# Decode attention with a gated FFN on one core: the output weights in three pieces instead of four, and unread matmuls moved

## The chip, the cores and the metric

The kernel runs on one core of a Trainium2 chip. The metric is the device time of one execution in microseconds; the time of a kernel is the median of several runs.

## What is computed

One decode step for two sequences: a layer norm, attention over the last 2048 positions of a cache, and a feed-forward network (FFN) whose output gates the attention's.

```
xn = layernorm(x)                                  # 2 x 1 x 448
q = (xn @ wq) -> 16 heads of 256
k, v = the last W = 2048 rows of the 8 kv heads, each used by 2 query heads
p = softmax(q k^T * 256**-0.5)
s = (p v) -> 2 x 1 x 4096 @ wo                     # wo is 4096 x 448
g = silu(relu(xn @ w1) @ w2)                       # 448 -> 1792 -> 448
out = x + s * g
```

Nearly all the bytes are the keys and values (eight loads of 4 MB), then wq and wo (3.67 MB each) and w1 and w2 (1.6 MB each).

## The kernel before, in words

Every engine has a list of operations written out by hand (`pr.op`, `pr.dma`); a wait stands in front of an operation only where it names another as a dependency. TensorE's list is cut into sections, which a small program of branches (L126 to L163) strings together: SA and SB (the scores), PV (probabilities times values), OT (the output turned), CH (the softmax chain), and at the end FFN, PV and OT once more, WO and END.

The work goes in four turns, k = 0 to 3. In each, the keys of one quarter of the heads are loaded (`load_k`), turned on VectorE in eight pieces (`do_T`, L460) and multiplied into the PSUM bank sbk by 32 matmuls (`do_S`). The softmax chain follows (L508 to L532), then 32 matmuls with the values (`do_PV`, into obk), a scaled copy to o_sb on ScalarE, and four small matmuls that turn it (`do_oT`).

All loads but two small ones are issued on SyncE's one queue, in the order wq, keys and values in turns, w1, w2, the last values, and then wo. wo goes into the buffer of the keys of turns 0 and 2 (`wo_sb = kbuf[0]`). A row of wo here is one of 32 slices: the 4096 rows are laid out as 128 partitions with 32 rows of 448 each, so that each of the 32 is one matmul's moving operand, 112 KB. `WO_PARTS` says in how many loads they come, `landed` which row has to wait for which load.

The end of the kernel, in TensorE's order: section FFN has two halves of the first product (`do_H`, 7 matmuls each into fbk and cbk), whose results VectorE takes through relu, a transpose and copies into h_sb (`do_hT`), and 14 matmuls with w2 (`do_F`); ScalarE and VectorE then make the gate g_sb (`do_gate`). The last PV and OT follow. In section WO two small matmuls fold the heads (`m_at`) and VectorE copies the result to at2. The first `WO_WIDE` rows of wo are multiplied wide: 448 columns each, four at a time in four strips of 32 columns of the array, so that four partial sums lie in wbk. VectorE copies wbk to wsum (L630), and four matmuls with `sel` add the four strips up into cbk. The remaining rows are multiplied narrow (`narrow`): each as four matmuls of 112 columns, in four strips, straight into cbk. The rows of the last load are in section END. Two VectorE operations multiply by the gate and add x, and ScalarE's queue stores the result.

`keep_busy(bank, n)` (L491) is a matmul in fp32 of the identity with n columns of itself, which runs as two matmuls. Nobody reads what it writes, and it waits for nothing: an unread matmul. Before the change there are such matmuls in each OT (256 columns, into wbk), behind the fold of the heads (512, into sbk), behind the first load's wide matmuls (384), and behind the last wide one (256).

Line 382 in the profile is the helper that makes all ordinary matmuls, L492 the unread ones, L46 the loads.

Of the kernel before, what the change touches and what calls it, by code (L numbers as in the profile page):

```python
# [165 lines left out]
def bass_recurrent_scan__sliding_block_cached__dense_activation_relu__decode_kernel(  # L166
# [24 lines left out]
    SLOTS = 7  # L191
    HC = HD // 2
    FC = DFF // 2
    WO_PARTS = [18, 6, 6, 2]
    WO_WIDE = 24
    NCOL = D // 4
    QW = 24 + 8 * 128
    BIG = 1e30
# [2 lines left out]
    with es:  # L201
# [5 lines left out]
        def psum(name, shape, dt):  # L207
            return es.enter_context(nc.psum_tensor(name, shape, dt))

        def view(t, off, dims, n=128, p0=0, pstep=1):  # L210
            width = t.shape[1]
            return bass.AP(t, p0 * width + off, [[width * pstep, n]] + dims)
# [55 lines left out]
        sbk = psum("sbk", [128, 512], F32)  # L268
# [112 lines left out]
        def mm(out_ap, lhsT, rhs, start, stop=False, **kw):  # L381
            return lambda e: e.matmul(out_ap, lhsT=lhsT, rhs=rhs, start=start, stop=stop,  # L382
                                      skip_group_check=True, **kw)
# [26 lines left out]
        def do_H(u):  # L410
            deps = [d_w1, v_xw] if u == 0 else []
            for s in range(SLOTS):
                lo = s * FC + u * (FC // 2)
                o = pr.op(PE, mm((fbk, cbk)[u][0:4, 0:FC // 2], xr[:, 4 * s:4 * s + 4], wbuf[:, lo:lo + FC // 2],
                                 s == 0, s == SLOTS - 1), deps)
                deps = []
            st["h_n"] = pr.op(DVE, lambda e: e.tensor_scalar(
                out=view(h_n, 32 * u, [[64, 14], [1, 32]], n=4), in0=view((fbk, cbk)[u], 0, [[1, 14], [14, 32]], n=4),
                scalar1=0.0, scalar2=None, op0=ALU.max), [o, p_z])

        def do_hT(u):
            v = pr.op(DVE, lambda e: e.transpose(
                view(ht, 32 * u, [[64, 14], [1, 32]], n=32), view(h_n, 32 * u, [[64, 14], [1, 32]], n=32)),
                [st["h_n"]])
            for hf in range(2):
                st["hT"] = pr.op(DVE, lambda e, hf=hf: e.tensor_copy(  # L426
                    view(h_sb, 0, [[1, 14], [16, 2]], n=32, p0=64 * hf + 32 * u),
                    view(ht, 32 * u + hf, [[64, 14], [2, 2]], n=32)), [v, p_z])

        def do_F():  # L430
            deps = [d_w2, st["hT"]]
            for f in range(14):
                lo = W2 + f * D
                o = pr.op(PE, mm(fbk[0:17, 0:D], h_sb[:, f:f + 17], wbuf[:, lo:lo + D], f == 0, f == 13), deps)
                deps = []
            st["F"] = o

        def do_gate():
            for i in range(4):
                a_e = pr.op(ACTE, lambda e, i=i: e.activation(  # L440
                    ea[32 * i:32 * i + 17, :], fbk[0:17, i * NCOL:(i + 1) * NCOL], ACT.Exp, scale=-1.0),
                    [st["F"], p_z])
            for i in range(4):
                a_g = pr.op(ACTE, lambda e, i=i: e.activation(
                    ga[32 * i:32 * i + 17, :], fbk[0:17, i * NCOL:(i + 1) * NCOL], ACT.Copy))
            v_d = pr.op(DVE, lambda e: e.tensor_scalar(
                out=ea[:, :], in0=ea[:, :], scalar1=1.0, scalar2=None, op0=ALU.add), [a_e])
            v_rc = pr.op(DVE, lambda e: e.reciprocal(tmp[:, :], ea[:, :]), [v_d])
            st["g"] = pr.op(DVE, lambda e: e.tensor_tensor(
                out=g_sb[:, :], in0=ga[:, :], in1=tmp[:, :], op=ALU.mult), [v_rc, a_g])  # L450
# [40 lines left out]
        def keep_busy(bank, n):  # L491
            pr.op(PE, lambda e: e.matmul(bank[:, 0:n], lhsT=ident_f[:, :],  # L492
                                         rhs=view(ident_f, 0, [[0, n // 128], [1, 128]]), start=True, stop=True))
# [100 lines left out]
        landed, j0 = {}, 0  # L594
        for n in WO_PARTS:
            landed[j0] = pr.dma(SP, wo_sb[:, j0 * D:(j0 + n) * D], wo_src[:, j0 * D:(j0 + n) * D],
# [5 lines left out]
        do_hT(0)  # L602
        do_H(1)
        do_hT(1)
        do_F()
        do_gate()
        pr.section("PV", NQ)
# [6 lines left out]
        for b in range(2):  # L614
            m_at = pr.op(PE, mm(mbk[:, 256 + 32 * b:288 + 32 * b], at_exp[:, 128 * b:128 * b + 128],
                                fold[:, :], b == 0, b == 1), deps)
            deps = []
        keep_busy(sbk, 512)
        v_at2 = pr.op(DVE, lambda e: e.tensor_copy(at2[:, :], mbk[:, 256:320]), [m_at])
        deps = [v_at2]  # L620
        for j in range(WO_WIDE):
            i = j % 4
            m_w = pr.op(PE, mm(wbk[32 * i:32 * i + 2, 0:D], view(at2, j, [[32, 2]]), wo_sb[:, j * D:(j + 1) * D],
                               j < 4, j + 4 >= WO_WIDE, tile_position=(0, 32 * i)), deps + [landed.get(j)])
            deps = []
            if j == WO_PARTS[0] - 1:
                keep_busy(sbk, 384)
            if j == WO_WIDE - 1:
                keep_busy(sbk, 256)
        v_ws = pr.op(DVE, lambda e: e.tensor_copy(wsum[:, :], wbk[:, 0:D]), [m_w])  # L630
# [11 lines left out]
        for i in range(4):  # L642
            pr.op(PE, mm(cbk[32 * i:32 * i + 17, 0:NCOL], sel[:, :], wsum[:, i * NCOL:(i + 1) * NCOL],
                         True, tile_position=(0, 32 * i)), deps)
            deps = []
        for j in range(WO_WIDE, 32):
            if j == max(landed):
# [39 lines left out]
```

## Time and profile before

| | |
|---|---|
| median of 3 runs | 110.13 us (109.85 to 110.47) |
| the profiled execution | 109.7 us, span of its instructions 108.4 us |
| mean granted clock of TensorE | 0.89 of full |
| busy: TensorE, VectorE, ScalarE, GpSimd | 69.6, 62.2, 14.9, 7.9 us |
| read from memory | 44.11 MB, 407 GB/s over the span |

The profile is of one execution; its times start at the span's first instruction. In a row of the timeline the columns are start, length, engine, line, operation, output and inputs with their shapes, and how many such instructions the row takes together; in brackets stands how long the engine was idle before it, and what ended that. A row of a table of stretches has the stretch and its length, then the busy time of PE, PEld, DVE, ACT and POOL with the number of instructions, the granted clock of TensorE, the busy share of the DMA engines and GB/s. In the list of DMA issues the last column is the median time from issue to landing.

### The profile page before, as it was taken

The numbers are of one execution on the slowest core, as the hardware profiler recorded it, in microseconds if no ns is written. First come the engines' busy times: TensorE is split into PE (matmuls) and PEld (weight loads), VectorE is DVE, ScalarE is ACT, GpSimd is POOL, SyncE is SP. The second block draws the span as 40 slices with busy tenths as digits, with TensorE's granted clock in tenths as the row PEclk, the third lists the DMA queues.
The fourth block names the chain that finished last, engine by engine and source line by source line (L and its number), as shares of the span: only waits on it lengthen the run. The fifth ranks groups of instructions, "written<-read, shape, count | busy, mean of one in ns | idle before, by whom it ended". The sixth has DMA issues, their size and how long they took to land.

```text
span 108.4 us, 1147 instructions
## 1 busy us (share of the span) xinstructions
PE 69.6 (64%) x432; PEld 27.4 (25%) x432; DVE 62.2 (57%) x106; ACT 14.9 (14%) x33; POOL 7.9 (7%) x31
## 2 busy tenths in 40 slices
PE   0000940059982999963799993169996597578891
PEld 0000200023421433432233332023432331223240
DVE  1679078099948999043999313299942216404022
ACT  2991000000003000203000023000002300045000
POOL 6500023000012000030000020000000000000000
PEclk9999999999999959999558999556999755999999
DMA  2999998899899998999889988998899998899970
GB/s 58 451 447 401 520 447 387 387 496 472 387 387 472 496 387 387 399 508 447 387 387 508 460 387 387 435 532 387 387 384 431 503 447 387 387 444 417 397 291 1
DMA packets 2332, 44.11 MB, mean 407 GB/s; under 512 B 282, under 2 KB 412, under 8 KB 668
## 3 DMA queue, kind: packets, MB, share of 16 engines
q1 hardware_dynamic: 2304, 44.11, 95.2%
q10 hardware_dynamic: 28, 0.01, 0.1%
HBM read 44.11 MB, written 0.00 MB: 407 GB/s over the span
## 4 chain that ended last, share of the span: by engine, by line
DMA 60%; PE 29%; DVE 5%; SPq 2%; issue 1%; ACT 1%; DVEq 0%; ACTq 0%
DMA kbuf<-in_A_k_cache_dram 42%; PE sbk L382 22%; DMA kbuf<-in_A_wo_dram 18%; PE obk L382 3%; DVE kt L460 2%; SPq L46 2%; PE wbk L382 1%; PE cbk L382 1%; PE sbk L492 1%; ACT e_sb L526 1%; DVE rm L508 1%; DVE wsum L630 1%; PE mbk L382 0%; PE nbk L382 0%; DVE mx L517 0%
## 5 line engine op out<-in xcount | busy, mean ns | idle before, releaser
L382 PE MATMUL sbk<-kt,qbd 128*128 128x512 bf16 x128 | 37.0, 456 | 12.7 <-DVE kt L460 12.7
L460 DVE STREAM_TRANSPOSE kt<-kbuf 128x1024 f32<-128x1024 f32 x32 | 36.7, 1206 | 6.8 <-DMA kbuf<-in_A_k_cache_dram 6.8
L382 PEld LDWEIGHTS sbk<-kt,qbd 128*128 128x128 bf16 x128 | 13.7, 111 | 35.3 <-issue 24.1
L382 PE MATMUL fbk<-wbuf,xq 128*4 128x512 bf16 x28 | 3.2, 624 | 10.9 <-DVE xq L369 10.9
L405 POOL COPY qbd<-qt 32x64 bf16<-32x64 bf16 x16 | 4.5, 284 | 54.4 <-PE sbk L382 42.5
L382 PE MATMUL obk<-vbuf,pt 128*16 128x512 bf16 x128 | 7.6, 379 | 0.8 <-DMA vbuf<-in_A_v_cache_dram 0.8
L488 ACT ACTIVATE o_sb<-obk,rs 128x512 bf16<-128x512 f32 x4 | 2.8, 688 | 37.5 <-PE obk L382 36.9
L508 DVE TENSOR_REDUCE rm<-sbk 128x1 f32<-128x512 f32 x4 | 2.8, 692 | 7.9 <-PE sbk L382 7.9
L525 ACT ACTIVATE bias<-mbk 128x1 f32<-128x1 f32 x4 | 0.7, 171 | 33.9 <-PE mbk L382 33.9
L382 PE MATMUL nbk<-ssum,gsum 128*128 128x1 f32 x8 | 1.7, 286 | 4.5 <-ACT e_sb L526 4.5
L531 DVE STREAM_TRANSPOSE pt<-e_sb 128x512 bf16<-128x512 bf16 x4 | 2.7, 687 | 3.2 <-ACT e_sb L526 3.2
L382 PEld LDWEIGHTS obk<-vbuf,pt 128*16 128x16 bf16 x128 | 2.8, 89 | 5.3 <-issue 1.3
L535 DVE TENSOR_TENSOR at_exp<-nbk,qmask 128x64 bf16<-128x64 f32 x4 | 0.9, 222 | 5.6 <-PE nbk L382 5.6
L382 PE MATMUL fbk<-wbuf,h_sb 128*17 128x448 bf16 x14 | 2.8, 352 | 2.0 <-DVE h_sb L426 2.0
L382 PEld LDWEIGHTS fbk<-wbuf,xq 128*4 128x4 bf16 x28 | 0.8, 107 | 12.4 <-issue 11.8
L382 PE MATMUL mbk<-one_f,mrow 1*128 1x1 f32 x8 | 1.5, 256 | 2.8 <-DVE mrow L520 2.8
L359 DVE TENSOR_SCALAR xg<-x_sb,st,rstd 2x384 bf16<-2x384 bf16 (+2 forms) x5 | 2.9, 603 | 0.1
L382 PE MATMUL cbk<-wbuf,xr 128*4 128x448 bf16 x7 | 2.8, 577 | 0.0
L526 ACT ACTIVATE e_sb<-sbk,bias 128x512 bf16<-128x512 f32 x4 | 2.7, 687 | 0.4
L382 PE MATMUL fbk<-wbuf,xr 128*4 128x448 bf16 x7 | 2.8, 571 | 0.0
L492 PE MATMUL sbk<-ident_f 128*128 128x512 f32 (+2 forms) x6 | 2.7, 534 | 0.0
L630 DVE COPY wsum<-wbk 128x448 f32<-128x448 f32 x1 | 0.6, 625 | 3.6 <-PE wbk L382 3.6
(85 smaller groups left out, 50.4 us busy)
## 6 DMA issues: line engine op xcount, KB each, us to landing
kbuf<-in_A_k_cache_dram SPq DMA_DIRECT2D x4, 4096.0 KB, 23.0
vbuf<-in_A_v_cache_dram SPq DMA_DIRECT2D x4, 4096.0 KB
wbuf<-in_B_w_dram SPq DMA_DIRECT2D x2, 1568.0 KB, 20.6
wbuf<-in_A_wq_dram SPq DMA_DIRECT2D x1, 2560.0 KB, 10.5
kbuf<-in_A_wo_dram SPq DMA_DIRECT2D x1, 2016.0 KB, 19.0
kbuf<-in_A_wo_dram SPq DMA_DIRECT2D x2, 672.0 KB, 20.7
wbuf<-in_A_wq_dram SPq DMA_DIRECT2D x1, 1024.0 KB, 4.8
kbuf<-in_A_wo_dram SPq DMA_DIRECT2D x1, 224.0 KB, 21.3
```

What stands on the lines that cost most here:

```text
L46: o = _Op(eng, lambda e: e.dma_start(dst, src), deps, True, key)
L359: xs["xn"] = pr.op(DVE, lambda e: e.tensor_scalar(out=view(xg, 128 + 128 * lo + shift, [[256, blocks], [128, 2], [pairs, 128 // pairs]], n=B),
L382: return lambda e: e.matmul(out_ap, lhsT=lhsT, rhs=rhs, start=start, stop=stop, skip_group_check=True, **kw)
L405: st["qbd", k] = pr.op(POOL, lambda e, a=a: e.tensor_copy(view(qbd, 24 + 32 * a, [[128, 8], [2, 4], [1, 2]], n=32, p0=32 * a), view(qt, 0, ...
L460: st["T", k, e] = pr.op(DVE, lambda e: e.transpose(view(dst, lo, [[128, NT // 2], [1, 32]]), view(src, lo, [[128, NT // 2], [1, 32]])), de ...
L488: st["osb", k] = pr.op(ACTE, lambda e: e.activation(o_sb[:, :], obk[:, :], ACT.Copy, scale=rs[:, k:k + 1]), [st["PV", k], st["rs", k]], ke ...
L492: pr.op(PE, lambda e: e.matmul(bank[:, 0:n], lhsT=ident_f[:, :], rhs=view(ident_f, 0, [[0, n // 128], [1, 128]]), start=True, stop=True))
L508: st["rm", k] = pr.op(DVE, lambda e: e.tensor_reduce(out=rm[:, :], in_=sbk[:, :], axis=AX.X, op=ALU.max), [st["S", k, 7]], key="rm")
L526: st["exp", k] = pr.op(ACTE, lambda e: e.activation(e_sb[:, :], sbk[:, :], ACT.Exp, bias=bias[:, 0:1], accum_out=ssum[:, 0:1]), [a], key=" ...
L531: st["pt", k] = pr.op(DVE, lambda e: e.transpose(pt[:, :], e_sb[:, :]), [st["exp", k]], key="pt")
L535: st["at", k] = pr.op(DVE, lambda e: e.tensor_tensor(out=view(at_exp, 16 * k, [[64, 4], [4, 4], [1, 4]]), in0=view(nbk, 0, [[4, 4], [1, 4] ...
L630: v_ws = pr.op(DVE, lambda e: e.tensor_copy(wsum[:, :], wbk[:, 0:D]), [m_w])
```

## The change

The loads of wo become three, of 22, 8 and 2 rows, and the 22 rows of the first are the wide ones; rows 22 and 23 become narrow. The unread matmul of 384 columns between the wide ones is gone. Behind the fold of the heads there are two unread matmuls of 512 columns instead of one, and two new ones, of 512 and 256 columns into sbk, stand in front of the second product of the FFN.

```
-    WO_PARTS = [18, 6, 6, 2]
-    WO_WIDE = 24
+    WO_PARTS = [22, 8, 2]
+    WO_WIDE = 22
...
         do_hT(0)
         do_H(1)
         do_hT(1)
+        for n in (512, 256):
+            keep_busy(sbk, n)
         do_F()
...
-        keep_busy(sbk, 512)
+        for n in (512, 512):
+            keep_busy(sbk, n)
         v_at2 = pr.op(DVE, lambda e: e.tensor_copy(at2[:, :], mbk[:, 256:320]), [m_at])
...
             deps = []
-            if j == WO_PARTS[0] - 1:
-                keep_busy(sbk, 384)
             if j == WO_WIDE - 1:
                 keep_busy(sbk, 256)
```

## The prediction, made before the changed kernel had run

> **What bounds the kernel now.** The page comes first: the slices of the span, the queues and the chain that ended last.
>
> ```profile
> span 108.4 us, 1147 instructions
> ...
> PEclk9999999999999959999558999556999755999999
> DMA  2999998899899998999889988998899998899970
> ...
> q1 hardware_dynamic: 2304, 44.11, 95.2%
> ...
> DMA 60%; PE 29%; DVE 5%; SPq 2%; issue 1%; ACT 1%; DVEq 0%; ACTq 0%
> ```
>
> The sixteen DMA engines are 80 to 90% busy or more from the second slice to the 38th, and one queue fills 95.2% of the span. So the stream of loads is the bound, and only what stands behind its last bytes can be shortened. The clock row shows 5s in four places: TensorE runs at half speed there. The chain in order of time shows the end.
>
> ```profile
> 82.78 19.04 DMA kbuf<-in_A_wo_dram
> 101.83 0.14 issue
> 101.96 1.11 PE wbk L382 x18
> 103.07 0.84 PE sbk L492 x2
> 103.92 0.49 PE wbk L382 x6
> 104.41 0.02 issue
> 104.43 0.64 DVE wsum L630
> 105.07 0.04 issue
> 105.11 0.94 PE cbk L382 x40
> ```
>
> The first wo piece lands at 101.83, 0.14 us later its 18 wide matmuls start, then come the unread 384, six wide, the copy to wsum and the narrow ones. The chain names a load once; whether a later piece also holds PE back, the issues and the narrow matmuls tell (the DMA list, the tile's own row, the timeline).
>
> ```profile
> kbuf<-in_A_wo_dram SPq DMA_DIRECT2D x1, 2016.0 KB, 19.0
> kbuf<-in_A_wo_dram SPq DMA_DIRECT2D x2, 672.0 KB, 20.7
> ...
> kbuf<-in_A_wo_dram SPq DMA_DIRECT2D x1, 224.0 KB, 21.3
> ```
>
> ```profile
> 83.89 0.91 SPq L46 DMA_DIRECT2D kbuf<-in_A_wo_dram  x2
> ```
>
> ```profile
> 105.32 0.48 PE L382 MATMUL cbk<-kbuf,at 128*17 128x112 bf16 x24
> ```
>
> ```profile
> 105.75 0.11 PEld L382 LDWEIGHTS cbk<-kbuf,at 128*17 128x17 bf16 x8
> 106.08 0.28 DVE L650 TENSOR_TENSOR tmp<-cbk,g_sb 128x112 f32<-128x112 f32 x1 [1.02 <-PE cbk L382]
> ```
>
> ```profile
> L382 PE MATMUL cbk<-kbuf,at 128*17 128x112 bf16 x32 | 0.7, 213 | 0.0
> ```
>
> The third and fourth issues end at 83.89 + 0.91 = 84.80. An issue is 0.43 us (the median in the tile's row, quoted below), so the fourth began at 84.37 and its two rows landed at 84.37 + 21.3 = 105.7. The 24 narrow matmuls ahead are six groups of four in 0.48 us, one matmul being 0.213, so a group follows the last by (0.48 - 0.21)/5 = 0.053. The seventh group would start at 105.32 + 6 x 0.053 = 105.64; it started at 105.75. **The end hangs on the last piece by 0.11 us**, and PE is that close behind it.
>
> **The change, part by part.**
>
> *Pieces.* Four loads of 18, 6, 6 and 2 rows become three of 22, 8 and 2: the same bytes. From 101.83 to 105.7 the last 14 rows take 3.87 us, 0.277 a row, three landings among them. The first 18 rows came from the landing of the last values, just ahead of PV:
>
> ```profile
> 97.03 1.90 PE L382 MATMUL obk<-vbuf,pt 128*16 128x512 bf16 x32 [0.78 <-DMA vbuf<-in_A_v_cache_dram]
> ```
>
> ```profile
> L46 SPq DMA_DIRECT2D kbuf<-in_A_wo_dram x4: 432/432/591, 82.8 to 84.4; - x4
> ```
>
> 101.83 - 97.0 = 4.83 us, 0.268 a row with one landing. With a cost c a piece and r a row, 18r + c = 4.83 and 14r + 3c = 3.87 give c = 0.05, r = 0.266. One piece less brings the last landing from 105.70 to 105.65 (bounds: 0, if c is only my rounding; and 0.12, if all that the 14 rows take over 14 x 0.268 = 3.75 belongs to the piece that goes; 0.05 lies nearest to the three landings sharing it). SP issues one load less, 0.43 us, at 83 to 85, over 12 us ahead of the data: worth nothing, since the queue is full until then.
>
> *Wide matmuls.* All 22 now wait for 22 rows: landing 101.83 + 4 x 0.266 = 102.9, start 0.14 later at 103.04. Groups of four: 18 are five groups in 1.11, six are two in 0.54 (rows below), so a group adds (1.11 - 0.54)/3 = 0.19, and six groups take 1.30: end 104.34.
>
> ```profile
> 101.96 1.11 PE L382 MATMUL wbk<-kbuf,at 128*2 128x448 bf16 x18 [0.44 <-DMA kbuf<-in_A_wo_dram]
> ...
> 103.00 0.91 PE L492 MATMUL sbk<-ident_f 128*128 128x384 f32 x2
> ...
> 103.85 0.54 PE L382 MATMUL wbk<-kbuf,at 128*2 128x448 bf16 x6
> ```
>
> Before they ended at 103.85 + 0.54 = 104.39. The unread 384 that goes lay between them (0.91) and was on PE's own chain; with it goes the split. So wsum starts 0.05 earlier, and the first narrow matmul at 105.27.
>
> *Narrow matmuls.* Rows 22 and 23 become narrow, two groups at 0.053. Rows 22 to 29 land at 102.9 + 8 x 0.266 + 0.05 = 105.08, before they are wanted. Rows 30 and 31 are the ninth group on: 105.27 + 8 x 0.053 = 105.69; their landing gives 105.65 + 0.05 = 105.70. PE and the load now arrive together, so the 0.11 of slack is spent, and the end moves from 105.75 to about 105.69: **-0.06 us**. Everything after 105.75 is as before.
>
> *Unread matmuls behind the fold.* One of 512 becomes two.
>
> ```profile
> 98.86 0.70 PE L492 MATMUL wbk<-ident_f 128*128 128x256 f32 x2
> ...
> 100.42 1.10 PE L492 MATMUL sbk<-ident_f 128*128 128x512 f32 x2
> 100.60 0.22 DVE L619 CAST at<-mbk 128x64 bf16<-128x64 f32 x1 [0.31 <-PE mbk L382]
> ```
>
> The operand at2 is there at 100.82, so the wide matmuls wait for the load alone. The pair runs from 100.42 to 102.6, and the 22 rows land at 102.9: at full clock it is hidden, with 0.3 us of cover. Queued behind it are the wide matmuls and all that follows.
>
> *Unread matmuls ahead of the FFN's second product.* 512 and 256 columns stand where PE waits for h_sb.
>
> ```profile
> 86.10 2.77 PE L382 MATMUL fbk<-wbuf,xr 128*4 128x448 bf16 x7
> ...
> 88.67 2.82 PE L382 MATMUL cbk<-wbuf,xr 128*4 128x448 bf16 x7
> ...
> 93.44 2.81 PE L382 MATMUL fbk<-wbuf,h_sb 128*17 128x448 bf16 x14 [1.95 <-DVE h_sb L426]
> ```
>
> They wait for nothing and can start at 88.67 + 2.82 = 91.49. (Seven products of this size take 2.77 at half clock, about 0.39 apiece, and fourteen 2.81 at full, 0.2.) At full clock they take 1.10 + 0.70 = 1.80 of the 1.95 gap: nothing. At half clock for all of it, 3.6, ending at 95.1, 1.65 after the product should start. Here the clock rises at 92.04, so 0.55 of the work is at half and the rest at full: 91.49 + 0.55 + (1.80 - 0.28) = 93.56 at most, 0.12 late, against 0.78 us in which PE waited for the values ahead of PV. I take nothing.
>
> *The clock.* What the unread matmuls could bring is speed after them. TensorE's granted clock in stretches between its own changes:
>
> ```profile
> 30.60:34.02 3.42, 1.88 (x9) 0.68 (x8) 1.36 (x4) 0.00 (x0) 0.96 (x4) 1.00 0.89 383
> 34.02:37.43 3.41, 2.27 (x11) 1.15 (x12) 3.41 (x5) 0.95 (x3) 0.00 (x0) 1.00 0.92 394
> 37.43:40.84 3.41, 3.41 (x9) 1.11 (x8) 3.41 (x4) 0.00 (x0) 0.00 (x0) 0.50 1.07 461
> ```
>
> ```profile
> 81.80:85.22 3.42, 1.75 (x17) 0.79 (x9) 0.63 (x3) 1.33 (x3) 0.00 (x0) 1.00 1.02 429
> 85.22:88.63 3.41, 3.05 (x9) 1.35 (x10) 0.77 (x2) 0.31 (x2) 0.00 (x0) 0.50 1.04 444
> 88.63:92.04 3.41, 2.85 (x8) 0.76 (x6) 2.20 (x5) 0.00 (x0) 0.00 (x0) 0.50 1.07 461
> 92.04:95.46 3.42, 2.02 (x11) 1.03 (x12) 1.17 (x4) 0.00 (x0) 0.00 (x0) 1.00 1.07 460
> ```
>
> The changes fall on a grid of 3.41 us. The clock fell after a stretch with 1.75 us of matmuls and stayed after 1.88 and 2.02; 2.27 before a fall shows that busy time is a rough gauge. From 92.04 to the end it stayed full. Were the grid some tenths earlier against the work, a stretch would hold the gap whole: 3.41 - 1.95 = 1.46 busy, and the clock would fall. PV and its neighbours would run at half for a while. Worst, the fall comes near 95.2: the last five products take 0.39 apiece instead of 0.2, ending 97.2, PV runs at half until 98.6 (0.7 of its 1.90 done) and ends at 99.8, 0.85 late. The old unread 512 would then end at 101.52 + 0.85 = 102.4, the 18 wide at 103.5, the unread 384 at 104.4, the six wide 0.47 later than before, and with 0.11 of slack the end would come 0.35 late. With the gap filled no such fall is left. Nothing ties the grid to the program's start in this trace, so some executions of before may pay 0 to 0.35; I take 0.15.
>
> [...]
>
> **Sum.** Against the profiled execution (109.7, span 108.4) the sum is -0.06: 109.64. That execution paid nothing for the clock after 92.04 and lies 0.43 below the median of 110.13 (109.85 to 110.47). Against the median I take -0.06 - 0.15: **109.9 us**.
>
> **Rivals.**
> 1. *The unread matmuls buy no clock at all* (the gap never dropped it): 110.13 - 0.06 = 110.07. For it: the traced execution had full clock from 92.04 on. [...]
> 2. *Clock falls are what sets the median apart from the profiled run*: then all 0.43 goes as well as the 0.06, and another 0.06 if c is at its upper bound: 109.6. For it: the bytes are the same in every execution, so something else makes the 0.62 us between runs. Against: the most that a fall costs is 0.35 by the sum above.
> 3. *The unread matmuls overrun* (slower). If the clock doesn't rise at 92.04 but a stretch later, near 95.7 with the grid shifted, the 768 columns end at 95.1, the product at 98.2 (95.1 + two at 0.39 + twelve at 0.2), PV starts 1.2 late, the pair behind the fold ends at 101.6 + 2.2 = 103.8 and the wide matmuls start at 103.85 for 103.04. The slack at the end is spent, so 0.8 - 0.06 = 0.74 comes through: 110.9. It decides once the pair ends after 102.9, that is when PV is over 0.3 late. For it: after 85.22 the clock needed two stretches, with 3.05 busy in the first. Against: 2.85 sufficed in the second.
> 4. *One load less, yet the end doesn't move*: narrow rows now sit on the path, and 0.1 to 0.2 lost anywhere in PE's tail shows: 110.3.
>
> **How the numbers follow.** Forecast 0.35 (own range 109.6 to 110.3), rival 1 0.2, rival 2 0.25, rival 3 0.15, rival 4 0.05. A half per cent is 0.55 us, about what a measurement of this kernel can tell from no change: under 109.58 is faster, over 110.68 slower. Rival 2 ends at that bound; with the 0.3 that the runs scatter to either side I count 0.18 of its 0.25 as faster, and 0.08 of the forecast's lower edge: 0.26. Slower is rival 3 with a little of rival 4: 0.16. Same: 0.58. The range takes in rival 2 with what spread the runs show, and rival 4 with as much; rival 3, at 0.15, is left out: 109.35 to 110.7.
>
> **What would show it.** The first wide matmul near 103.04, right behind its load and with idle PE before it; were it behind the unread pair without idle time, rival 3 holds. The last eight narrow matmuls at about 105.69. Full clock from about 92 to the end. The product of the FFN starting within 0.15 of h_sb. An end that moves by over 0.3 us in the span while the last landing doesn't would prove the sum wrong.

## The result, and the profile after

| | before | after |
|---|---|---|
| median of 13 executions | 110.13 us (109.85 to 110.83) | 110.94 us (109.91 to 113.17) |
| the profiled execution | 109.7 us | 110.66 us |
| its span | 108.4 us | 108.3 us |
| its time outside the span | 1.3 us | 2.36 us |

The ratio is 1.005, with an interval of 1.0027 to 1.0073: slower, and 1.04 us above the forecast of 109.9. (The ratio and its interval, here and below, leave out executions of over 1.5% above a kernel's fastest; these are three of 13 of the changed kernel, of 112.7 to 113.2 us, four of 12 in e8, three of 12 in e11, and one or none in each other experiment's kernel.)

The table holds the surprise: the span of the changed kernel is shorter, as forecast, and its time is longer. What was lost lies where the profile has no instruction.

First the changed kernel's page: span, granted clock, queues and the shares of the chain.

```profile
span 108.3 us, 1166 instructions
...
PEclk9999999999999959999558999556999755999999
...
q1 hardware_dynamic: 2160, 44.11, 95.4%
q8 instruction: 1, 0.02, 0.1%
...
DMA 61%; PE 28%; DVE 5%; SPq 2%; issue 1%; ACT 1%; DVEq 0%; ACTq 0%
```

Against the page of before: the same bytes on q1, the same chain of loads, half clock in the same four places, 19 more instructions, and one row that before did not have: a queue named "instruction" moved one packet. In the trace's list of packets it begins at 107.19, is 16,384 bytes and takes 0.93 us on one DMA engine; no other packet of that size and queue is there, and before has none. From the queue's name it is taken below for a block of instructions, and its transfer for a fetch.

The changed kernel's chain in order of time (start, length, what):

```profile
82.73 20.08 DMA kbuf<-in_A_wo_dram
102.81 0.14 issue
102.94 1.32 PE wbk L382 x22
104.26 0.02 issue
104.28 0.64 DVE wsum L631
104.92 0.04 issue
104.96 0.98 PE cbk L382 x48
105.94 0.02 issue
105.96 0.29 DVE tmp L651
```

Its wo loads in the list of DMA issues (size, time to landing):

```profile
kbuf<-in_A_wo_dram SPq DMA_DIRECT2D x1, 2464.0 KB, 20.1
...
kbuf<-in_A_wo_dram SPq DMA_DIRECT2D x1, 896.0 KB, 21.7
kbuf<-in_A_wo_dram SPq DMA_DIRECT2D x1, 224.0 KB, 21.7
```

The load of 22 rows lands at 102.81, all 22 wide matmuls run in one piece behind it, and the last operation but one (tmp) starts at 105.96 where before it started at 106.08: 0.12 earlier. The same in the timeline (start, length, engine, line, operation; idle time and releaser in brackets):

```profile
91.36 1.86 PE L492 MATMUL sbk<-ident_f 128*128 128x512 f32 x4
...
93.39 2.81 PE L382 MATMUL fbk<-wbuf,h_sb 128*17 128x448 bf16 x14 [0.17 <-DVE h_sb L426]
...
100.36 1.96 PE L492 MATMUL sbk<-ident_f 128*128 128x512 f32 x4
...
102.94 1.30 PE L382 MATMUL wbk<-kbuf,at 128*2 128x448 bf16 x22 [0.62 <-DMA kbuf<-in_A_wo_dram]
...
104.28 0.62 DVE L631 COPY wsum<-wbk 128x448 f32<-128x448 f32 x1 [3.51 <-PE wbk L382]
```

And the last eight narrow matmuls, by their weight loads, in a view of that moment:

```profile
105.63 0.11 PEld L382 LDWEIGHTS cbk<-kbuf,at 128*17 128x17 bf16 x8
```

The unread matmuls fit into both gaps: 91.36 + 1.86 ends just ahead of the FFN's product, and 100.36 + 1.96 = 102.32 leaves PE idle for 0.62 us before the wide matmuls. The two stretches of the clock's grid that hold the filled gaps keep full clock:

```profile
92.01:95.42 3.41, 3.24 (x15) 1.41 (x14) 1.15 (x4) 0.00 (x0) 0.00 (x0) 1.00 1.07 461
98.83:102.25 3.42, 2.89 (x16) 1.16 (x12) 0.45 (x2) 0.69 (x1) 0.00 (x0) 1.00 0.91 388
```

So nothing inside the span explains the 0.81 us between the medians. Each execution is listed with its span; time less span is the part outside. Over the changed kernel's 13 executions its median is 2.40 (1.51 to 2.69), with spans of 108.3 to 108.5 in ten and 110.3 to 110.5 in three. The kernel before ran beside the experiments 123 times on four chips; there its part outside has medians of 1.35 to 1.45 and a lowest value of 1.27, and 25 of the 123 lie between 1.9 and 2.6.

### The profile page after: what moved, and what is told of

It reads as the page before. It is cut to its first block, busy times and chain, and to the rows that moved or that the text cites. A ratio compares the mean times of both kernels' runs of the same rounds, so it can differ in the third digit from the quotient of the medians.

```text
span 108.3 us, 1166 instructions
## 1 busy us (share of the span) xinstructions
PE 71.2 (66%) x442; PEld 28.5 (26%) x442; DVE 62.2 (57%) x106; ACT 14.9 (14%) x33; POOL 7.8 (7%) x31
## 4 chain that ended last, share of the span: by engine, by line
DMA 61%; PE 28%; DVE 5%; SPq 2%; issue 1%; ACT 1%; DVEq 0%; ACTq 0%
DMA kbuf<-in_A_k_cache_dram 42%; PE sbk L382 22%; DMA kbuf<-in_A_wo_dram 19%; PE obk L382 3%; DVE kt L460 2%; SPq L46 2%; PE wbk L382 1%; PE cbk L382 1%; ACT e_sb L526 1%; DVE rm L508 1%; DVE wsum L631 1%; PE mbk L382 0%; PE nbk L382 0%; DVE mx L517 0%; DVE tmp L651 0%
## 5 line engine op out<-in xcount | busy, mean ns | idle before, releaser
L382 PE MATMUL sbk<-kt,qbd 128*128 128x512 bf16 x128 | 37.0, 456 | 12.6 <-DVE kt L460 12.6
L382 PEld LDWEIGHTS sbk<-kt,qbd 128*128 128x128 bf16 x128 | 13.7, 111 | 35.2 <-issue 24.4
L382 PE MATMUL fbk<-wbuf,xq 128*4 128x512 bf16 x28 | 3.2, 626 | 11.0 <-DVE xq L369 11.0
L382 PE MATMUL obk<-vbuf,pt 128*16 128x512 bf16 x128 | 7.6, 379 | 0.8 <-DMA vbuf<-in_A_v_cache_dram 0.8
L382 PE MATMUL nbk<-ssum,gsum 128*128 128x1 f32 x8 | 1.7, 286 | 4.5 <-ACT e_sb L526 4.5
L492 PE MATMUL sbk<-ident_f 128*128 128x512 f32 (+1 forms) x10 | 4.5, 566 | 0.0
L382 PEld LDWEIGHTS obk<-vbuf,pt 128*16 128x16 bf16 x128 | 2.8, 89 | 5.3 <-issue 1.3
L382 PEld LDWEIGHTS fbk<-wbuf,xq 128*4 128x4 bf16 x28 | 0.8, 107 | 12.4 <-issue 11.8
L382 PE MATMUL mbk<-one_f,mrow 1*128 1x1 f32 x8 | 1.5, 256 | 2.8 <-DVE mrow L520 2.8
L382 PE MATMUL fbk<-wbuf,h_sb 128*17 128x448 bf16 x14 | 2.8, 352 | 0.2 <-DVE h_sb L426 0.2
L382 PE MATMUL cbk<-wbuf,xr 128*4 128x448 bf16 x7 | 2.8, 577 | 0.0
L382 PE MATMUL fbk<-wbuf,xr 128*4 128x448 bf16 x7 | 2.8, 571 | 0.0
L492 PE MATMUL wbk<-ident_f 128*128 128x256 f32 x8 | 2.7, 417 | 0.0
```

## The theories and the experiments

**Theory 1, instructions.** The change makes TensorE's program longer, and its trace has a packet of 16,384 bytes that before does not have. The author's guess from these two is that beyond some length a further block of instructions is fetched near the end, and the execution ends later by that. Counted in the compiled program, where an ordinary matmul is two instructions (weights, then data) and one in fp32 is four, TensorE's program goes from 441 to 461 (on the pages PE and PEld go from 432 to 442 each): 8 for the two unread matmuls in front of the FFN's second product, 4 for the one more behind the fold, 4 less for the one of 384 columns, and 12 for two rows that become narrow (four matmuls each instead of one). With one load less on SP that is the page's 1147 to 1166.

**Theory 2, unread matmuls** (rival): they cost by themselves, by running late in some executions or by taking something from the end. **Theory 3, pieces** (rival): 22 rows land too late, or the narrow rows hold up the end, in executions that the profile didn't show.

All kernels were timed in five rounds beside the kernel before. Instructions called dead are never executed. In each heading stands the number of TensorE's instructions. "Outside" is the median of time less span.

### e1: before with 20 dead instructions (461)

```
-            nc.br("all_end", engines=only)
+            nc.br_eq(reg, 16, on_true="pe_dead", on_false="all_end", engines=only)
+        with nc.body("pe_dead", valid_engines=only):
+            for _ in range(9):
+                self.filler(t)        # matmul of 32 columns, never reached
+            nc.br("all_end", engines=only)
...
+        pr.filler = lambda e: e.matmul(sbk[:, 0:32], lhsT=ident[:, :], rhs=ident[:, 0:32], start=True, stop=True)
```

> Before, with 20 TensorE instructions more that are never executed: 9 small matmuls behind the last section, jumped over by a branch. Nothing of the change is in it. Theory 1 (length): the change made TensorE's program 20 instructions longer (461 for 441), the end of it falls into another 16 KB block of instructions, and fetching that block costs time behind the span. Then this kernel loses as the change does: span as before (108.4), time 0.4 to 1 us over before, and a packet of 16384 bytes on an instruction queue near the end. Theory 2 (the unread matmuls) and theory 3 (the pieces of wo): no difference from before, within 0.2 us.

Measured: 110.89 beside 110.34, ratio 1.0045 (1.0015 to 1.0076). Outside 1.90 beside 1.45. The instruction queue's packet is there, at 107.41. Instructions that never run cost about as much in the ratio as the whole change, and 0.45 us outside the span where the change costs 1.0: for theory 1, and neither rival can make it.

This execution also shows what the gap ahead of the FFN's second product can do in the kernel before. Two stretches of e1's table between changes of the clock:

```profile
90.53:93.94 3.41, 1.40 (x8) 0.48 (x7) 2.76 (x7) 0.00 (x0) 0.00 (x0) 1.00 0.89 384
93.94:97.36 3.42, 3.42 (x12) 1.25 (x10) 0.00 (x0) 0.00 (x0) 0.00 (x0) 0.50 0.92 395
```

The clock's grid has edges at 90.53 and 93.94 where the trace of before had them at 88.63, 92.04 and 95.46. So one stretch holds the gap whole, with 1.40 us of matmuls, and the clock falls behind it.

### e2: before with ten small unread matmuls that do run (461)

```
+        for _ in range(10):
+            pr.op(PE, lambda e: e.matmul(sbk[:, 0:32], lhsT=ident[:, :], rhs=ident[:, 0:32], start=True, stop=True))
         do_F()
```

> Before, with ten small unread matmuls (32 columns, 20 instructions) in front of the FFN's second product, where TensorE idles for 1.95 us. They take about 0.3 us and add nearly no busy time. Theory 1 (length): as the unexecuted ones, 0.4 to 1 us over before, with the packet at the end. Theory 2 (the busy time of the unread matmuls, through the clock or the order behind them): no difference within 0.2 us. Theory 3 (pieces): no difference.

Measured: 111.36, 1.0074 (1.0041 to 1.0106), outside 2.38, packet at 108.41. As e1, and with the changed kernel's own part outside (2.40).

### e3: after without the unread matmuls in front of the FFN's second product (453)

```
-        for n in (512, 256):
-            keep_busy(sbk, n)
         do_F()
```

> After, without the two unread matmuls in front of the FFN's second product: 453 instructions. Theory 1 (length): if the block's border lies between 453 and 461, the loss is gone and the time is 0.1 under before; if it lies lower, all of the loss stays. Theory 2 with these two as the cause: the loss is gone. Theory 3 (pieces): the loss stays, 0.5 us over before.

Measured: 110.33, 1.0001 (0.997 to 1.0032), outside 1.46, no packet. Eight instructions fewer and the loss is gone, although the pieces and the pair behind the fold are as in the changed kernel: theory 3 falls for those. Theory 2 could still claim this run, since unread matmuls went. But what their absence did inside the span is the opposite of a gain. Stretches of e3:

```profile
89.81:93.22 3.41, 1.29 (x7) 0.42 (x5) 3.22 (x8) 0.00 (x0) 0.00 (x0) 1.00 1.05 452
93.22:96.63 3.41, 3.27 (x9) 1.26 (x10) 0.00 (x0) 0.00 (x0) 0.00 (x0) 0.50 0.93 398
96.63:100.04 3.41, 3.41 (x40) 1.63 (x38) 1.09 (x3) 2.12 (x9) 0.00 (x0) 1.00 0.97 416
```

And its timeline:

```profile
93.36 4.41 PE L382 MATMUL fbk<-wbuf,h_sb 128*17 128x448 bf16 x14 [2.25 <-DVE h_sb L426]
...
101.33 1.96 PE L492 MATMUL sbk<-ident_f 128*128 128x512 f32 x4
...
103.41 1.30 PE L382 MATMUL wbk<-kbuf,at 128*2 128x448 bf16 x22
```

The open gap dropped the clock, the product took 4.41 instead of 2.81, the pair behind the fold ended at 101.33 + 1.96 = 103.29, and the wide matmuls came right behind it without a wait for their load, 0.47 later than in the changed kernel. The span is 108.7 for 108.3.

### e4: after with pieces of 24, 6 and 2 rows, 24 wide (449)

```
-    WO_PARTS = [22, 8, 2]
-    WO_WIDE = 22
+    WO_PARTS = [24, 6, 2]
+    WO_WIDE = 24
```

> After, with wo in pieces of 24, 6 and 2 and 24 rows wide, so that two rows are two instructions each and not eight: 449 instructions, all unread matmuls of the change kept. Theory 1 (length): the loss is gone if the border lies above 449; the wide matmuls then start 0.55 later than in after and the end moves by up to 0.4 for it. Theory 2 (unread): the loss stays, 0.5 over before at the least. Theory 3 (pieces, three of them): the loss stays.

Measured: 110.65, 1.0017 (0.9993 to 1.0042), outside 1.33, no packet. All unread matmuls of the change are in it, with twelve instructions fewer, and the part outside is 1.33 beside 1.45 for before: theory 2 falls for the part outside. Its spans are 108.8 to 109.5: the wide matmuls now start at 104.00, behind 1.15 us of idle time, a loss of its own.

### e5, e6: before with 60 and with 16 dead instructions (501, 457)

The lines that differ from e1:

```
-            for _ in range(9):
+            for _ in range(29):       # e6: 7
```

> Before, with 60 instructions that are never executed behind TensorE's last section: 501 in all. If the loss is a step (one more block to fetch, Theory 1), it is as large as with 20: 0.45% over before, within 0.2 us of it, and the packet of 16384 bytes is there. If every instruction of length costs (a longer load of the program ahead of the span, say), it is three times that, 1.4%.

> Before, with 16 instructions that are never executed: 457 in all, between the 453 that lost nothing and the 461 that lost. A step gives either nothing (no packet) or the whole 0.45% (with the packet), and nothing in between; a cost by length gives 0.35%.

Measured: e5 111.62 beside 110.43, 1.0082 (1.0051 to 1.0114); e6 110.52, 0.9998 (0.9975 to 1.0021). The step lies between 457 and 461, so it is a step and no price per instruction. Two things don't fit a simple picture. e6 has a packet on the instruction queue too, at 107.64, and loses nothing (outside 1.44). And e5 loses only 0.39 outside the span (1.75 beside 1.36), but its spans are 0.85 longer (109.85 beside 109.0 at the median). Its trace has two such packets, at 107.79 and at 111.27, the second 0.73 us behind the end of the span: here a packet is seen in the part outside.

What ended the profiled span, 110.5 and the longest of the 12, stands in the trace's list of instructions (the views of the profile leave jumps out). TensorE's last jump, behind section END, begins at 106.77 and takes 3.77 us; it ends at 110.55, and the span ends with it, where SyncE's wait for the store was over at 109.51. The same jump takes 0.38 in e1 and e6. The store of the output is not what ended late: its packets run from 109.02 to 109.11, 1.23 us behind its issue, and in before they begin 1.23 us behind it too. So in e5 TensorE itself waits at a jump, and the first packet is moved during that wait. In e1 the jump is as short as in e6, so e1's loss lies behind it.

### e7: e5 with its last jump announced ahead (504)

```
         with nc.body("pe_wo", valid_engines=only):
+            hint2 = t.mark_branch_hint_location()
...
+            nc.br_eq(reg, 16, on_true="pe_dead", on_false="pe_end2", engines=only)
+        with nc.body("pe_end2", valid_engines=only):
+            t.br("pe_last").branch_hint(hint2)
...
+        with nc.body("pe_last", valid_engines=only):
```

The jump to the program's last body is announced where section WO begins, which was to bring the packet forward; the dead instructions stand between.

> The 60 unexecuted instructions again, and a prefetch hint at the beginning of section WO for the last branch, over them (504 in all). Theory 1, if it is the late fetch that costs: the packet of 16384 bytes moves from behind 107 to about 100 us, beside other work, and most of the loss goes (within 0.2 us of before). If the fetch isn't what costs, or can't be brought forward in this way, the time is that of the 60 without the hint.

Measured: 110.41 beside 110.43, 0.9982 (0.9947 to 1.0017), outside 1.33. The announcement runs at 100.15, the first packet moves from 107.79 to 105.17, and the whole loss of e5 is gone with three instructions more than e5 has. So the length by itself doesn't cost. TensorE's last jump takes 1.69 us here, but it ends at 107.70, ahead of the end of the span at 108.49, where e5's ended at 110.55. A second packet begins at 108.55, behind the span, and costs nothing, so a late packet as such doesn't cost. The reading that fits is that TensorE has to wait for one at the end. The trace shows that wait in e5; for the other kernels that lose it is argued.

### e8: after with one unread matmul of 512 ahead of the product and one behind the fold (453)

```
-        for n in (512, 256):
+        for n in (512,):
             keep_busy(sbk, n)
         do_F()
...
-        for n in (512, 512):
-            keep_busy(sbk, n)
+        keep_busy(sbk, 512)
```

> After, with one unread matmul of 512 in front of the FFN's second product and one behind the fold, instead of two each: 453 instructions, the pieces of 22, 8 and 2 kept. Theory 1: no packet, and what the change was worth by the sum shows: 0.1 to 0.2 us under before, or 0.998. Theories 2 and 3: between after and before, 0.2 us or more over before.

Measured: median 111.28 (110.13 to 113.15), 1.0017 (0.9975 to 1.0059), outside 1.44. Outside as theory 1 has it; the spans are another matter: 108.5 to 110.4, and 109.7 or more in seven of 12. The profiled one is such an execution. Its stretches:

```profile
100.29:103.70 3.41, 1.47 (x12) 0.58 (x16) 0.45 (x2) 0.09 (x1) 0.00 (x0) 1.00 0.92 386
103.70:107.12 3.42, 3.42 (x24) 1.16 (x24) 0.62 (x1) 0.00 (x0) 0.00 (x0) 0.50 0.36 140
```

And its timeline:

```profile
101.08 1.10 PE L492 MATMUL sbk<-ident_f 128*128 128x512 f32 x2
103.66 2.40 PE L382 MATMUL wbk<-kbuf,at 128*2 128x448 bf16 x22 [1.48 <-DMA kbuf<-in_A_wo_dram]
105.99 1.22 PE L492 MATMUL sbk<-ident_f 128*128 128x256 f32 x2
```

With one unread matmul, PE waits 1.48 us for the 22 rows; the stretch holds 1.47 us of matmuls, the clock falls just as the rows land, and the wide matmuls take 2.40 for 1.30, on the path to the end. Here, behind the last wait for a load, a fall costs.

### e9: after with 60 dead instructions and the announced jump (524)

The edit is e7's, made to the changed kernel.

> After, unchanged in its work, with the 60 unexecuted instructions behind the last section and the hint at the beginning of section WO for the branch over them (524 instructions). If the late fetch is what the change lost (theory 1), the time outside the span falls from after's median of 2.40 us to about 1.35, as it did when the 60 stood behind before, though the program is longer still; the time is that of before or 0.1 to 0.3 under it, except for executions in which the clock falls while PE waits for the 22 rows. If the loss is of another kind, the time outside the span stays over 2 and the ratio at 1.005.

Measured: 109.96 beside 110.38, 0.997 (0.9929 to 1.0011), outside 1.31 (1.27 to 1.35 over 12 executions), packet at 105.07. Its page:

```profile
span 108.8 us, 1169 instructions
...
q8 instruction: 1, 0.02, 0.1%
```

The changed kernel, 63 instructions longer still, without its loss: 1.1 us of the part outside is gone while the instruction queue still moves a block of that size.

### e10: before's pieces with the change's unread matmuls in both places (453)

```
+        for n in (512, 256):
+            keep_busy(sbk, n)
         do_F()
...
-        keep_busy(sbk, 512)
+        for n in (512, 512):
+            keep_busy(sbk, n)
```

> Before with the unread matmuls of the change in both places, pieces and wide rows as before (453 instructions). Theory 1: nothing outside the span (1.35 to 1.45). For the clock: with the gap ahead of the FFN's second product filled, its clock fall is gone, and spans lie closer together at the lower end of before's (108.4 to 108.9 for 108.4 to 109.6): 0.998. If the unread matmuls overrun, the 512 more behind the fold end at 102.6, after the 18 rows have landed at 101.83, and the span is 0.3 to 0.6 longer, since all the wide ones and the 384 stand behind them.

Measured: 110.68 beside 110.38, 1.0028 (0.9988 to 1.0067), outside 1.48. Its timeline:

```profile
100.53 1.96 PE L492 MATMUL sbk<-ident_f 128*128 128x512 f32 x4
102.42 0.93 PE L382 MATMUL wbk<-kbuf,at 128*2 128x448 bf16 x15
```

Without the larger first piece the pair overruns the landing of 18 rows: no idle time ahead of the wide matmuls, which start 0.46 later than in the trace of before. The unread matmuls alone bring no gain that can be measured. Theory 2's loss outside the span isn't there either (1.48 beside 1.35); the interval of the whole time is too wide to tell.

### e11: the pieces alone (449)

```
-    WO_PARTS = [18, 6, 6, 2]
-    WO_WIDE = 24
+    WO_PARTS = [22, 8, 2]
+    WO_WIDE = 22
...
-            if j == WO_PARTS[0] - 1:
-                keep_busy(sbk, 384)
```

> Before with the pieces of 22, 8 and 2, 22 rows wide and no 384, and the unread matmuls otherwise as before (449 instructions). Nothing outside the span by theory 1. PE idles from 101.5 to 103 for the 22 rows, 0.85 us longer than in after: if idle time there makes the clock fall in some executions, more of them than in after (3 of 13) have spans of about 110.3, as the kernel with 453 instructions had with one unread 512 there; otherwise spans are as before less 0.06.

Measured: 110.49 beside 110.38, 0.9977 (0.9936 to 1.0018), outside 1.33, no packet. Theory 3 falls for the part outside. In its trace the clock was at half from 93.45 to 96.86, so the gap did it here too, and the span was 108.4 all the same. Over the 12 executions the spans run from 108.3 to 110.4, and in three they are 110.0 or more: long executions come with the pieces alone, about as often as in the changed kernel.

### e12: after with 256 columns more behind the fold, 60 dead and the announced jump (528)

The edit is e9's, with (512, 512, 256) behind the fold. It was to end what e8 shows: more matmuls in PE's wait for the 22 rows.

> After with 256 more unread columns behind the fold (512, 512 and 256), the 60 unexecuted instructions and the hint (528). The three end near 102.95 where the 22 rows land at 102.8 to 102.9, so PE idles for less than 0.1 us there. If idle time at this place is what lets the clock fall, no execution has a span near 110.3 any more, at the price of at most 0.15 us on the others; and the time outside the span is 1.35. Together 0.997 of before. If the falls come from elsewhere, 2 or 3 of 12 remain.

Measured: 111.27 beside 110.38, 1.0079 (1.005 to 1.0109), outside 1.52, spans 109.4 to 110.5 beside 108.4 to 110.1. A miss: the idle time ahead of the wide matmuls is filled (0.20 left), and everything is about a us later. The packets stand at 35.59 and 111.26, the first in the middle of the kernel.

### e13, e14: after with the announced jump alone (463); after with the 256 columns alone (465)

e13:

```
         with nc.body("pe_wo", valid_engines=only):
+            hint2 = t.mark_branch_hint_location()
...
+            t.br("pe_last").branch_hint(hint2)
+        with nc.body("pe_last", valid_engines=only):
             nc.br("all_end", engines=only)
```

e14:

```
-        for n in (512, 512):
+        for n in (512, 512, 256):
```

> After with the hint at the beginning of section WO for the last branch, and no unexecuted instructions (463). If what has to be fetched early is the block that the last branch goes to, and that block begins before the branch's target, the time outside the span falls to 1.3 as with the 60 between; if the target lies in a block that is there anyway and the late fetch is of the one behind it, the hint fetches nothing new and the time outside the span stays at 2.4.

> After with 512, 512 and 256 unread columns behind the fold and nothing else (465 instructions): the run with 528 instructions again without its length. If idle time ahead of the wide matmuls lets the clock fall, no span near 110.3 is left and spans lie at 108.3 to 109.0; time outside the span 1.9 to 2.4 as in the other kernels past 457, so the median stays 0.5 to 1 us over before. If the 1.0 us that the kernel with 528 instructions lost in its span comes from the 256 columns and not from its length, spans are near 109.8 here too.

Measured: e13 110.25 beside 110.47, 0.9985 (0.9953 to 1.0018), outside 1.31 (1.28 to 1.39). e14 (seven executions) 111.24, 1.0067 (1.0035 to 1.01), outside 1.31, spans 109.6 to 110.0. So e13 frees the changed kernel of its loss with two instructions, and e14 has its loss in the span. e13's page has two packets:

```profile
span 108.9 us, 1168 instructions
...
q8 instruction: 2, 0.03, 0.1%
```

The first begins at 105.07, the second at 108.31, and that one lasts until 109.35, past the end of the span, and costs nothing. The last jump waits here too, 1.31 us, and is through at 107.59.

Where e14 loses, the timelines tell. The first PV in e13 (L385 is the helper that is L382 in the other rows shown):

```profile
41.42 1.91 PE L385 MATMUL obk<-vbuf,pt 128*16 128x512 bf16 x32 [0.60 <-DMA vbuf<-in_A_v_cache_dram]
```

The same and the wide matmuls in e14:

```profile
42.30 1.90 PE L382 MATMUL obk<-vbuf,pt 128*16 128x512 bf16 x32 [0.64 <-DMA vbuf<-in_A_v_cache_dram]
...
104.45 1.30 PE L382 MATMUL wbk<-kbuf,at 128*2 128x448 bf16 x22 [0.20 <-DMA kbuf<-in_A_wo_dram]
```

And e14's page:

```profile
span 109.9 us, 1170 instructions
...
q8 instruction: 2, 0.03, 0.1%
```

In e14 a packet begins at 35.39 and takes 1.07 us on one DMA engine, amid the loads (500 GB/s from 35 to 37 us, 459 from 37 to 39); the values that the first PV waits for land 0.88 later than in e13, and the lateness stays to the end (the wide matmuls at 104.45, in e13 at 103.56). The second packet, at 107.94, costs nothing outside the span. The packet's time on one engine and the delay are of one size (1.07 and 0.88); that the loads land late because the one engine was taken is the author's guess, and wasn't tried by itself. Why e12 and e14 have a packet there, and kernels of 461 to 463 and 501 to 524 instructions do not, stays open; in these two alone TensorE's first jump behind section SB, at 30.75 and 31.26, takes 0.37 us; in the fourteen other traces it takes 0.23.

## Why the prediction was wrong

**The bound and the pieces: right.** The load of wo still ends last. 22 rows landed about 102.8 (forecast 102.9), the wide matmuls started at 102.94 (103.04), took 1.30 (1.30) and ended at 104.24 (104.34), the last eight narrow matmuls at 105.63 (105.69). The end moved by -0.12 (tmp at 105.96 for 106.08) where the sum had -0.06; the other half is no merit of the pieces, for the last PV, ahead of them, already starts 0.06 earlier in this trace (96.97 for 97.03).

**The unread matmuls: right.** Both sets are hidden: the product starts 0.17 behind h_sb (within 0.15 was forecast, so 0.02 over), the pair ends 0.62 ahead of the wide matmuls. Rival 3's overrun at half clock doesn't show in the changed kernel's trace. Three of its 13 executions have spans of 110.3 to 110.5, and their cause stays open. e8 shows a clock fall in the wait for the 22 rows that makes just such spans, but the clocks on record speak against it here: the mean granted clock of these three is 0.892. A span times the share of the clock that was missing, divided by 1.71 (half of a stretch of 3.41), is the number of stretches at half clock: 7.0 in all three, as in the profiled execution (108.3 at 0.89) and never fewer in the other ten (7 to 10, all with spans of 108.3 to 108.5). A fall at the end would be one more, unless one was missing earlier.

**The clock: the mechanism right, the gain unproven.** The grid does shift against the work between executions (edges at 90.53 in e1 and 89.81 in e3, at 88.63 and 92.04 in before), and the gap of 1.95 does drop the clock in some: e1, e3 and e11 each show it, after stretches with 1.29 and 1.40 us of matmuls in the two quoted. In e11 it cost nothing, since PE's wait for the 22 rows covered it (span 108.4). What it costs with the pieces of before, for which the 0.35 was worked out, no run separates. With the last jump announced the changed kernel stands at 0.997 (e9) and 0.9985 (e13); the forecast of -0.21 in 110 is 0.998. Both intervals include 1, so the gain is neither shown nor excluded. The spans don't settle it: 108.3 to 108.5 in ten executions of the changed kernel, 108.65 and 108.9 at the median in e9 and e13, and 108.9 to 109.0 at the median for before. A stretch need not be idle for a fall behind it: those in e1, e3 and e8 were 38 to 43% busy.

**The step that failed: "Everything after 105.75 is as before",** and with it the carrying of the sum over to the median as if what lies around the span were a constant. It was 1.3 in the profiled execution of before and 2.36 in that of after, and over the executions 1.35 to 1.45 against 2.40. The term is missing from the sum and was worth +1.0 us. TensorE's program passed from 441 instructions to 461; between 457 (e6, no loss) and 461 (e1 and e2, 0.45 and 0.74%) lies the step; instructions that never run make it (e1, e5); announcing the last jump a section earlier, with which a packet begins at 105.07 to 105.17, takes it away (e7, e9, e13). None of the four rivals was of this kind: all looked for the loss between 88 and 106.

The instruction count of the added operations stood in none of the terms. The runs show 0.4 to 1.0 us more outside the span in the kernels that lose there (e1, e2, e5 and the changed one). Of these, one shows a wait, e5 with its last jump of 3.77 us; in e1 the same jump takes 0.38.

**The second fault was the reading of the 0.43** by which the profiled execution of before lay under its median. It was put down to the clock (0.15, or all of it in rival 2). The kernel before scatters outside the span as well, from 1.27 to 2.6 over 123 executions, with spans from 108.4 to 110.1, so part of the 0.43 may lie outside the span; the spans of the runs behind the 110.13 are not on record. A table of time, span and difference for each run would have shown that there is such a term.

**What stays open.** Packets on the instruction queue are in traces without a loss (e6 at 457, e8 and e10 at 453; a second one at 108.55 in e7, 108.31 in e13 and 107.94 in e14), so neither the packet nor its late moment is by itself the mark of the loss. Why the step lies between 457 and 461 instructions is not shown. How the fetch, which ends at 108.1 in the changed kernel's trace, makes the part outside a us longer isn't shown either: the kernel has no jump on record behind section END, so a wait like e5's would stand behind TensorE's last recorded instruction. In e5 and e12, whose profiled executions have 1.9 and 2.16 us outside, a further packet begins 0.7 and 1.3 us behind the end of the span; in the changed kernel's trace no such packet was recorded.

No version beats the kernel before for certain: the changed kernel with the announced jump (e9, e13) is the best found, clearly ahead of the changed kernel in the part outside (1.31 against 2.40), and level with the kernel before within the intervals.

## What to carry to other kernels

Set the time of the profiled execution beside its span, before and after: a loss outside the span is not to be found in any chain of waits, and the sum of a prediction has to have a term for it. When an edit adds operations, count instructions of that engine as well as microseconds (two for an ordinary matmul, four for one in fp32 here), and look at the page for an instruction queue; here 461 instructions for 457 cost 0.45% (e1 beside e6), about 0.5 us, where the edit moved the end by 0.12. A jump announced a section early, with the packet at 105.07 for 107.19, took the cost away here for two instructions (e13, 1.31 us outside the span for 2.40). And where a span grows without a wait in any view, look at the jumps in the list of instructions, as e5 shows.

## What was not expected of the hardware

- Twenty instructions that are never executed cost 0.45% (e1), sixteen nothing (e6). With sixty, TensorE's last jump took 3.77 us and ended the span (e5).
- One block of 16,384 bytes takes 0.93 to 1.36 us on one DMA engine. At the end of the program it comes with up to 1.0 us more outside the span, or with nothing (e6, e13); fetched at 35.4 us, amid a full stream of loads, it comes with spans that are 0.9 us longer (e14, 109.9 beside 109.0 at the median); fetched at 105.1, behind nearly all loads, it costs nothing (1.31 us outside the span in e9 and e13).
- The clock fell after stretches of 3.41 us that were not idle but held 1.29 (e3), 1.40 (e1) and 1.47 us (e8) of matmuls; the prediction's rows have it fall after 1.75 and 2.27 too and stay after 1.88 and 2.02. Over all sixteen traces, of the stretches at full clock every one with 1.72 us or less was followed by a fall (56), every one with 2.28 or more was not (162), and in between both happened (18 falls, 12 not). A fall costs next to nothing ahead of a wait for a load (e11, span 108.4 as in before) and 1.1 us on the wide matmuls behind the last one (e8, 2.40 for 1.30).
